# Another order of the units of a fused attention and gated-MLP kernel, with other PSUM tiles and copying engines

## The chip, the cores and the metric

One core of one Trainium2 chip runs the kernel. The metric is device time in microseconds (us); less is better. It has five instruction queues that matter here: TensorE (PE; PEld is its weight load), VectorE (DVE), ScalarE (ACT), GpSimd (POOL) and SyncE (SP, which only issues transfers). Each runs its own instructions in the order in which the program issues them.

## What is computed

An attention over blocks (batch 4, 8 heads, 768 rows in 8 blocks of 96, head size 64) is followed by a gated MLP with a spatial product. Cut to what matters:

```python
P = sort_net                                   # [4, 8, 8, 8]
for _ in range(5):                             # Sinkhorn rounds
    P = np.exp(P - np.max(P, axis=-1, keepdims=True))
    P = P / (np.sum(P, axis=-1, keepdims=True) + 1e-09)
    P = P / (np.sum(P, axis=-2, keepdims=True) + 1e-09)
k_sorted = np.einsum('bhij,bhjcd->bhicd', P, k_b)      # blocks mixed by P
v_sorted = np.einsum('bhij,bhjcd->bhicd', P, v_b)
attn = softmax(q_b @ k_sorted^T / 8)                   # each block with its own
x = (attn @ v_sorted), heads side by side              # [4, 768, 512]
h = np.maximum(x @ w_in, 0.0)                          # [.., 1024]
u, v = h[..., :512], h[..., 512:]
v_n = (v - mean(v)) / sqrt(var(v) + 1e-06)
v_s = np.einsum('ts,bsd->btd', w_spatial, v_n) + b_spatial[None, :, None]
out = (u * v_s) @ w_out                                # fp32
```

## The kernel before

The kernel is a list of small units. A table, ORDER (line 18 on), names them one after the other; `run` (line 806) takes each item, splits it at the colons and calls the function `u_<name>` with the rest as arguments. Nothing is scheduled afterwards: what a unit issues goes to its engines' queues in the order of the table. A unit on TensorE takes the number of a PSUM tile (`ps_tile`, line 110: 0 to 3 in use are pairs of banks, 10 to 17 are the single banks in these pairs) and a letter for the engine that copies its result away, D for VectorE and A for ScalarE. The next unit on the same tile waits for that copy.

The units, by what they do for one batch b (each batch goes through all of it; the table interleaves the MLP of one batch with the attention of the next):

- L loads q, k, v or a weight on GpSimd's queue (lines 177 to 194): `L:q:2:0:8` is q of batch 2, `L:wv` and `L:wu` are the two halves of w_in, `L:wsa` and `L:wsb` the row tiles 0 to 2 and 3 to 5 of w_spatial, `L:wo` is w_out; BI loads b_spatial spread over the partitions (line 206). Half of the first q comes in fp32 on SyncE's queue (LH, line 360) and is cast by QC (line 367).
- SK is a Sinkhorn round (lines 248 to 261): one exponential on ScalarE, six small steps on VectorE. PR, PC, P0 and PD spread its result into the mixing matrix pd.
- KT and VT mix k and v by it and turn them (L395); VM mixes v without a turn (L422), and VC copies vm to vb, one block a transfer, on SyncE's queue (L435); VB is the turn for batch 0.
- QT turns q on TensorE (L326). For batches 2 and 3, QP rearranges it (L377, a copy) and QX turns it with a transfer on SyncE's queue (L382).
- SC makes scores (L454) and their exponentials on ScalarE (L459); AT multiplies with v (L500) and divides on VectorE (L507, L508) into x. XT turns x on TensorE, XD with a transfer on SyncE's queue (L518).
- VP and VH make the v half of h for 128 rows (L567) with a relu (L128 or L130), ST its statistics (L587, L588), LN the root on ScalarE, LA the normalised v (L599). UP makes a piece of u (L613).
- WT and WW turn one and two row tiles of w_spatial (L536, L543). SP is the spatial product (L625, sum z with b_spatial on VectorE, L631), GT the product with u (L642, on VectorE or GpSimd), OP the output product (L651), OE its copy out of PSUM, OS the store (L666).
- SH, GH, OH, OI and OJ are the same steps in smaller pieces for the last batch (L681 to L719). CK and CF test whether the fast path's numbers were in range and write a flag; LF reads it into a register on every engine (L752). Behind the item IF stands a branch on it (line 815): the usual side runs the last output products, the other a safe path over everything.

`L:wsb` is thus needed first by the first WT or WW of a row tile from 3 to 5, `L:wu` by the first UP, and the whole of w_spatial and b_spatial by the first SP. What the reader has to know of the calls:

```python
for item in order.split():
    name, *args = item.split(":")
    units[name](*args)
```

Of the kernel before, what the change touches and what calls it, by code (L numbers as in the profile page):

```python
# [15 lines left out]


ORDER = """
S0 TB CO LH:S:0 L:q:0:4:8 SK:0 DM:10:3:384 DM:10:4:512 DM:10:13:512 BH ID IV:0 L:v:0:0:8 MC MA SK:1 DM:10:4:256 SK:2
QC:A:0 SK:3 SK:4 QC:A:1 QT:10:A:0:2 IV:2 QT:11:A:0:3 DM:12:4:512 QT:12:A:0:0 DM:13:10:192 PR:10 MB P0:0:2 P0:2:4  # L20
QT:11:D:0:1 VT:2:A:0:0 VT:3:D:0:1 PC:A P0:4:6 P0:6:8 VB:13:A:0:0 VB:12:D:0:1 L:k:0:0:8 VT:2:A:0:2 KT:3:D:0:1
KT:1:A:0:2 KT:0:A:0:3 VT:2:D:0:3 SC:3:0:1:1 KT:1:D:0:0 SC:0:0:2:0 VB:14:D:0:2 SC:3:0:3:0 L:k:1:0:8 AT:1:0:1:1
SC:0:0:0:0 L:v:1:0:8 PD:1:0:4 VB:15:D:0:3 SC:3:0:1:0 AT:1:0:2:0 SC:0:0:2:1 AT:2:0:3:0 SC:3:0:0:1 PD:1:4:8 AT:1:0:0:0
KT:0:A:1:0 XT:14:D:0:0:2 AT:3:0:0:1 SC:1:0:3:1 KT:0:A:1:3 AT:2:0:2:1 VM:1:A:1:0 AT:3:0:3:1 VM:0:A:1:1 VM:2:D:1:3
L:q:1:0:8 VM:1:A:1:2 XT:16:A:0:1:2 L:wv AT:0:0:1:0 XT:17:A:0:1:0 KT:2:D:1:1 KT:1:A:1:2 QT:16:D:1:1 QT:10:D:1:3
QT:11:A:1:2 QT:17:D:1:0 XT:14:D:0:0:0 SC:1:1:1:0 L:wsa SC:0:1:2:1 SC:3:1:2:0 VP:15:D:0:4 ST:0:4 VP:14:D:0:3 L:wu
SC:1:1:0:0 SC:0:1:1:1 VP:15:D:0:1 L:wsb ST:0:3 WT:16:A:1 WT:17:D:0 VP:14:A:0:0 ST:0:1 VH:15:A:0:2 ST:0:0 WT:16:A:2
VC:1:0:4 L:q:2:0:8 VH:17:A:0:5 VC:1:4:8 PD:2:0:4 ST:0:2 ST:0:5 AT:1:1:0:0 LN:0:0:6 AT:0:1:1:0 UP:2:A:0:0:0
UP:3:A:0:1:0 BI LA:0:3 LA:0:4 AT:1:1:2:0 SC:2:1:0:1 UP:0:A:0:1:1 LA:0:1 AT:3:1:2:1 L:v:2:0:8 WT:14:A:3 L:k:2:0:8
LA:0:5 LA:0:2 WW:1:D:4 LA:0:0 SC:0:1:3:1 SC:3:1:3:0 UP:2:A:0:0:1 PD:2:4:8 AT:0:1:3:1 QP:A:2:0 SP:1:0:3 QP:A:2:3  # L30
AT:3:1:3:0 QP:A:2:2 AT:2:1:0:1 QP:A:2:1 SP:0:0:0 AT:1:1:1:1 SP:3:0:2 VM:2:A:2:2 XD:1:0 VM:0:A:2:1 GT:D:0:0 SP:1:0:1
VM:3:D:2:0 GT:P:0:1 VM:2:A:2:3 VH:10:A:1:0 ST:1:0 KT:1:A:2:0 KT:2:D:2:1 KT:3:A:2:3 QX:2:0:4 KT:0:D:2:2 XD:1:1
UP:1:A:1:1:0 VH:16:D:1:1 SC:2:2:2:0 SC:0:2:0:0 VC:2:0:4:0:4 ST:1:1 GT:P:0:2 SC:1:2:3:0 VH:17:D:1:3 L:wo UP:2:A:1:1:1
AT:0:2:2:0 VH:16:A:1:4 AT:1:2:0:0 GT:P:0:3 VH:17:D:1:5 SC:2:2:1:0 L:q:3:0:8 SC:0:2:0:1 SC:1:2:1:1 VH:16:A:1:2 ST:1:3
UP:2:A:1:0:0 ST:1:5 AT:0:2:3:0 ST:1:4 ST:1:2 UP:1:A:1:0:1 LN:1:0:6 OP:3:0:2:2 LA:1:5 LA:1:1 SC:2:2:3:1 L:v:3:0:8
SC:0:2:2:1 PD:3:4:8 LA:1:0 OP:1:0:4:2 PD:3:0:4 LA:1:3 LA:1:2 OE:A:0:2 LA:1:4 L:k:3:0:8 QP:D:3:0 VC:2:4:8:0:4 OE:A:0:4
AT:2:2:3:1 SP:0:1:3 QP:A:3:3 AT:3:2:1:0 AT:1:2:2:1 QP:A:3:1 SP:2:1:1 AT:0:2:1:1 QP:A:3:2 VM:3:A:3:1 OP:1:0:0:2
OE:D:0:0 OS:0:0:0:1:A OS:0:0:1:2:A VM:2:A:3:3 AT:3:2:0:1 SP:0:1:2 VM:1:A:3:0 GT:P:1:1 XD:2:0 VM:3:D:3:2 SP:2:1:0
VH:16:D:2:2 QX:3:0:4 KT:0:A:3:0 KT:1:D:3:2 KT:2:D:3:3 KT:3:A:3:1 XD:2:1 VH:10:D:2:0 SC:1:3:0:1 ST:2:2 SC:3:3:0:0
SC:2:3:3:1 VC:3:4:8:0:4 OS:0:4:0:1 OS:0:4:1:2 VH:11:D:2:4 VH:10:A:2:5 AT:1:3:0:1 GT:P:1:3 VH:16:D:2:3 ST:2:3 ST:2:5  # L40
GT:P:1:2 SC:2:3:1:1 SC:0:3:2:1 SC:1:3:1:0 VH:17:A:2:1 GT:D:1:0 UP:2:A:2:1:0 AT:0:3:2:1 UP:1:A:2:1:1 ST:2:1 AT:3:3:1:1
ST:2:4 AT:2:3:3:1 UP:0:A:2:0:1 ST:2:0 UP:1:A:2:0:0 VC:3:0:4:0:4 AT:3:3:0:0 LN:2:0:6 LA:2:2 OP:0:1:0:2 OE:A:1:0 LA:2:4
AT:2:3:1:0 OP:1:1:4:2 LA:2:5 SC:3:3:2:0 LA:2:0 LA:2:3 LA:2:1 SC:0:3:3:0 OP:2:1:2:2 AT:3:3:3:0 SP:0:2:1 GT:D:2:1
OE:A:1:4 XD:3:1 AT:1:3:2:0 SP:3:2:0 SP:0:2:2 CK XD:3:0 GT:P:2:0 OE:A:1:2 SP:2:2:3 VH:1:D:3:5:3 GT:D:2:3 VH:10:D:3:4
UP:3:A:3:1:1 CF:11 VH:12:A:3:2 VH:13:A:3:1 OS:1:2:0:1 OS:1:2:1:2 LF VH:16:A:3:0 GT:D:2:2 OS:1:0:0:1:A OS:1:0:1:2:A
UP:2:A:3:1:0 ST:3:1 ST:3:3 UP:0:A:3:0:0 ST:3:4 ST:3:5 OP:1:2:0:2 ST:3:2 ST:3:0 OP:3:2:4:2 LN:3:0:6 LA:3:3 OE:D:2:0
LA:3:4 OP:2:2:2:2 LA:3:0 LA:3:1 OE:A:2:2 LA:3:5 UP:0:A:3:0:1 OE:A:2:4 LA:3:2 OS:0:2:0:1 OS:0:2:1:2 SH:12:3:2:0
SH:13:3:3:0 GH:P:3:3:0 SH:16:3:0:0 GH:D:3:2:0 SH:17:3:1:0 GH:P:3:0:0 SH:16:3:1:1 SH:12:3:2:1 OS:2:4 GH:P:3:1:0
SH:13:3:3:1 OS:2:0 GH:D:3:1:1 SH:17:3:0:1 OS:1:4 GH:D:3:3:1 OS:2:2 GH:P:3:0:1 GH:P:3:2:1 IF OH:16:3:2:0:512:0:4
OI:A:3:2:0:512 OH:12:3:3:0:512:0:4 OH:13:3:0:0:512:0:4 OI:D:3:0:0:512 OI:A:3:3:0:512 OH:17:3:1:0:512:0:4  # L50
OJ:3:2:0:512:S OJ:3:3:0:512:A OI:A:3:1:0:512 OJ:3:0:0:512:S OH:16:3:4:256:512:0:4 OI:D:3:4:256:512 OH:12:3:5:0:256:0:4
OI:D:3:5:0:256 OJ:3:1:0:512:S OJ:3:4:256:512:A OH:13:3:5:256:512:0:4 OJ:3:5:0:256:S OI:D:3:5:256:512
OH:17:3:4:0:128:0:4 OH:10:3:4:128:256:0:4 OI:B:3:4:0:256 OJ:3:5:256:512:A OJ:3:4:0:256:S
"""


# [792 lines left out]
```

## Time and profile before

| what | value |
|---|---|
| time, median of 3 runs | 150.17 us (149.5 to 150.21) |
| span of the profiled execution | 147.7 us, 4114 instructions |
| granted TensorE clock, mean | 1.000 |
| TensorE busy | 141.4 us, 96% of the span |
| VectorE / ScalarE / GpSimd busy | 115.1 / 85.2 / 39.1 us |
| chain that ended last, by engine | PE 82%, DMA 8%, DVE 5%, POOL 2% |
| read from HBM / written to it | 24.78 MB / 6.29 MB |

The page gives the profiled execution's span, from its first to its last instruction; the time of the runs has what lies around that too. The chain is followed back from the last instruction, at each step to what released it. Matmuls are pipelined, so a busy TensorE need not be at its peak. A load is told by its issue on the queue and by its time from there to landing.

### The profile page before, as it was taken

How to read it: one execution, taken by the hardware profiler on the slowest of the kernel's cores; microseconds unless marked ns; L12 is line 12 of the kernel's file. 1: busy time of each engine (PE TensorE's matmuls, PEld its weight loads, DVE VectorE, ACT ScalarE, POOL GpSimd, SP SyncE). 2: the span in 40 equal slices, each digit the busy share in tenths (PEclk: the TensorE clock that was granted, in tenths of full speed). 3: DMA queues.
4: the chain of work that ended last, by engine and by line, in shares of the span. 5: the costliest groups of instructions: out<-in, count | busy, mean ns of one | idle time of the engine just before them, and what ended most of it. 6: DMA issues, size and time to landing. Idle time of an engine off the chain costs nothing.

```text
span 147.7 us, 4114 instructions
## 1 busy us (share of the span) xinstructions
PE 141.4 (96%) x1691; PEld 101.0 (68%) x1691; DVE 115.1 (78%) x263; ACT 85.2 (58%) x125; POOL 39.1 (26%) x44
## 2 busy tenths in 40 slices
...
GB/s 60 278 204 205 204 207 201 208 225 243 227 233 231 204 200 269 131 177 211 206 202 175 213 239 278 132 0 83 28 0 60 190 2 284 0 2 266 307 210 228
DMA packets 37013, 25.93 MB, mean 176 GB/s; under 512 B 16704, under 2 KB 34112, under 8 KB 36992
## 3 DMA queue, kind: packets, MB, share of 16 engines
...
HBM read 24.78 MB, written 6.29 MB: 210 GB/s over the span
## 4 chain that ended last, share of the span: by engine, by line
PE 82%; DMA 8%; DVE 5%; POOL 2%; issue 1%; ACT 1%; POOLq 0%; DVEq 0%
PE ps L625 16%; PE ps L567 15%; PE ps L613 14%; PE ps L651 11%; DMA k_in<-in_k_dram 8%; PE ps L681 5%; PE ps L500 4%; PE ps L395 4%; PE ps L701 4%; PE ps L454 4%; PE ps L422 3%; DVE x_sb L508 2%; PE ps L326 1%; PE ps L536 1%; PE ps L530 1%; DVE vb L124 1%
## 5 line engine op out<-in xcount | busy, mean ns | idle before, releaser
L642 POOL TENSOR_TENSOR gt<-z,u_sb 128x768 bf16<-128x768 f32 x7 | 11.4, 1642 | 68.0 <-DVE z L631 54.7
L459 ACT ACTIVATE ex_all<-ps 96x768 bf16<-96x768 f32 x32 | 23.7, 805 | 5.0 <-PE ps L454 4.1
L625 PE MATMUL ps<-wspT,v_sb 128*128 128x384 bf16 x144 | 25.0, 326 | 0.0
L567 PE MATMUL ps<-w_in_sb,xT 128*128 128x256 bf16 (+1 forms) x176 | 23.8, 283 | 0.0
L613 PE MATMUL ps<-xT,w_in_sb 128*128 128x384 bf16 x128 | 23.0, 326 | 0.0
L128 ACT ACTIVATE u_sb<-ps 128x768 bf16<-128x768 f32 x16 | 13.0, 811 | 17.3 <-PE ps L613 17.2
L508 DVE TENSOR_TENSOR x_sb<-ps,rec_all 96x512 bf16<-96x512 f32 x32 | 22.0, 687 | 1.1
L625 PEld LDWEIGHTS <-v_sb 128*128 128x128 bf16 x144 | 13.5, 98 | 8.4
L567 PEld LDWEIGHTS <-xT 128*128 128x128 bf16 x176 | 16.2, 98 | 4.0
L651 PE MATMUL ps<-w_out_sb,gt 128*128 128x256 bf16 x144 | 16.9, 273 | 0.0
L613 PEld LDWEIGHTS <-w_in_sb 128*128 128x128 bf16 x128 | 12.0, 98 | 7.0
L587 DVE BATCH_NORM_STATS2 stats<-v_sb 128x6 f32<-128x512 bf16 x24 | 16.2, 675 | 0.6 <-ACT v_sb L128 0.5
L122 ACT COPY o_sb<-ps 128x1024 f32<-128x1024 f32 (+2 forms) x11 | 8.9, 830 | 12.6 <-PE ps L701 9.3
L631 DVE TENSOR_TENSOR z<-ps,b_bc 128x768 f32<-128x768 f32 x12 | 11.5, 954 | 5.9 <-PE ps L625 5.1
L651 PEld LDWEIGHTS <-gt 128*128 128x128 bf16 x144 | 13.8, 98 | 2.0
L500 PEld LDWEIGHTS <-ex_all 96*128 96x128 bf16 x256 | 11.1, 97 | 2.6
L500 PE MATMUL ps<-vb,ex_all 96*128 96x65 bf16 x256 | 12.4, 193 | 0.1
L122 ACT CAST vm<-ps 128x768 bf16<-128x768 f32 x9 | 6.8, 807 | 9.7 <-PE ps L422 6.6
L694 POOL TENSOR_TENSOR gt<-z,u_sb 128x512 bf16<-128x512 f32 (+1 forms) x5 | 5.2, 1046 | 21.5 <-DVE z L687 21.5
L507 DVE RECIPROCAL rec_all<-ps 96x8 f32<-96x8 f32 x32 | 6.3, 196 | 5.5 <-PE ps L500 5.3
L130 DVE TENSOR_SCALAR v_sb<-ps 128x512 bf16<-128x512 f32 (+1 forms) x12 | 8.7, 727 | 1.7 <-PE ps L567 1.5
L236 PE MATMUL ps<-warm 128*128 128x512 bf16 (+3 forms) x38 | 8.5, 386 | 1.3 <-DVE warm L210 1.3
...
## 6 DMA issues: line engine op xcount, KB each, us to landing
v_in<-in_v_dram POOLq DMA_DIRECT2D x4, 768.0 KB, 16.0
k_in<-in_k_dram POOLq DMA_DIRECT2D x4, 768.0 KB, 14.9
vb<-vm SPq DMA_DIRECT2D x24, 99.0 KB, 4.8
q_in<-in_q_dram POOLq DMA_DIRECT2D x3, 768.0 KB, 11.6
...
out_dram<-o_sb SPq DMA_DIRECT2D x4, 512.0 KB, 5.9
...
ws_in<-in_moe_w_spatial_dram POOLq DMA_DIRECT2D x2, 576.0 KB, 18.9
```

The lines of the kernel that those rows point to most:

```text
L122: nc.scalar.copy(out=out, in_=in_)
L128: nc.scalar.activation(out=out, in_=in_, func=AF.Relu)
L459: nc.scalar.activation(out=e_tile(b, hp, ih).rearrange("p h (x g) -> p h x g", g=G), in_=t[0:BLK, :, 0:HW].rearrange("p h (g x) -> p h x g ...
L500: nc.tensor.matmul(t[:, hh, ii * VW:ii * VW + D + 1], lhsT=e[:, c:c + 128], rhs=vb[b % 2][:, ih * NI + ii, 2 * hp + hh, 0:D + 1], start=Tr ...
L508: nc.vector.tensor_mul(out=x_sb[:, hp].rearrange("p i (h d) -> p h i d", h=2), in0=tv[:, :, :, 0:D], in1=_raw_ap(rec, 0, [rec.ap[0], [NI, ...
L567: nc.tensor.matmul(t[:, x, c:c + DH // parts], lhsT=st["xT", b][:, n // 3, kc, (n % 3) * 128:(n % 3 + 1) * 128], rhs=w_in_sb[:, kc, DH + c ...
L587: nc.vector.bn_stats(out=stats, in_=st["v_sb", b, n])
L613: nc.tensor.matmul(t[:, x, 0:HW], lhsT=w_in_sb[:, kc, mc * 128:(mc + 1) * 128], rhs=st["xT", b][:, ih, kc, :], start=(kc == 0), stop=(kc = ...
L625: nc.tensor.matmul(t[:, x, 0:HW], lhsT=st["v_sb", b, n][:, mc * 128:(mc + 1) * 128], rhs=wspT[:, 3 * x:3 * x + 3, n, :], start=(n == 0), s ...
L631: nc.vector.tensor_add(out=z.rearrange("p (x c) -> p x c", x=2), in0=t[:, :, 0:HW], in1=b_bc.rearrange("p (x c) -> p x c", x=2),)
L642: eng.tensor_mul(out=gt, in0=st["z", b, mc], in1=u)
L651: nc.tensor.matmul(t[:, x, c:c + w], lhsT=st["gt", b, mc][:, (n0 + x) * 128:(n0 + x + 1) * 128], rhs=w_out_sb[:, mc, c:c + w], start=(mc = ...
```

## The change

The change rewrites the table ORDER and nothing else: the same 385 items, with the same work in each, in another turn, with other tile numbers and other letters for the copying engine. Counted over the table, the two casts QC go from ScalarE to VectorE; VectorE copies four of the eight QP (one before), three of the sixteen UP (none), seven VH (nine), four VM (three), and six KT (seven); GpSimd multiplies ten of the twelve GT (seven) and three of the eight GH (five). The table fills most of the diff; this is its core, with the QC casts, the first u unit (UP) and the first use of `L:wsb` (WW in the new table, WT:14:A:3 in the old one, a little ahead of WW there):

```diff
@@ -16,41 +16,41 @@
...
-QC:A:0 SK:3 SK:4 QC:A:1 QT:10:A:0:2 IV:2 QT:11:A:0:3 DM:12:4:512 QT:12:A:0:0 DM:13:10:192 PR:10 MB P0:0:2 P0:2:4
...
-SC:1:1:0:0 SC:0:1:1:1 VP:15:D:0:1 L:wsb ST:0:3 WT:16:A:1 WT:17:D:0 VP:14:A:0:0 ST:0:1 VH:15:A:0:2 ST:0:0 WT:16:A:2
-VC:1:0:4 L:q:2:0:8 VH:17:A:0:5 VC:1:4:8 PD:2:0:4 ST:0:2 ST:0:5 AT:1:1:0:0 LN:0:0:6 AT:0:1:1:0 UP:2:A:0:0:0
...
+QC:D:0 SK:3 QT:12:A:0:3 QC:D:1 SK:4 IV:2 DM:12:4:512 QT:16:A:0:2 DM:13:10:192 QT:14:A:0:1 PR:10 MB P0:2:4 P0:0:2
...
+VP:15:A:0:3 SC:1:1:2:0 SC:0:1:0:0 ST:0:3 SC:3:1:1:1 WT:14:D:2 VP:15:D:0:0 PD:2:0:4 WT:13:A:1 ST:0:0 VH:11:A:0:2
+AT:2:1:3:0 AT:3:1:2:0 UP:0:A:0:0:1 AT:1:1:1:0 PD:3:4:8 VH:15:A:0:5 ST:0:2 QP:D:2:2 L:wsb VP:17:A:0:1 ST:0:5 SC:2:1:2:1
...
+WW:2:A:4 LA:0:4 AT:3:1:0:1 WT:11:D:3 LA:0:0 WT:10:A:0 UP:1:A:0:1:0 BI LA:0:2 QP:A:2:1 AT:3:1:2:1 L:k:2:0:8 AT:2:1:0:0
...
```

The first place is GpSimd's queue, from the two loads of w_spatial to the k of batch 2 (ws_in is half of w_spatial, L185 the u half of w_in, q_in, v_in and k_in are those of batch 2, pd is the mixing matrix):

```order
 L191 DMA ws_in<-in_moe_w_spatial_dram 128x3x768
 L185 DMA w_in_sb<-in_moe_w_in_dram 128x4x512
+L177 DMA q_in<-in_q_dram 128x8x384
+L293 TENSOR_TENSOR pd<-mask_89,prep_sb 128x512 x2
 L191 DMA ws_in<-in_moe_w_spatial_dram 128x3x768
-L177 DMA q_in<-in_q_dram 128x8x384
 L293 TENSOR_TENSOR pd<-mask_89,prep_sb 128x512
+L177 DMA v_in<-in_v_dram 128x8x384
 L206 DMA b_bc<-in_moe_b_spatial_dram 128x768
-L177 DMA v_in<-in_v_dram 128x8x384
 L177 DMA k_in<-in_k_dram 128x8x384
```

The load of q of batch 2 moved from behind the second half of w_spatial to ahead of it, and v of batch 2 from behind b_spatial to ahead of it.

The second place is SyncE's queue around the transfers of batch 2 (xT is the turned x of batch 1, qT the turned q of batch 2, the copies to vb above it are those of batch 1, those below of batch 2):

```order
 L435 DMA vb_98<-vm 96x1x528 x8
-L518 DMA_TRANSPOSE xT<-x_sb 128x16x96
+L518 DMA_TRANSPOSE xT<-x_sb 128x16x96 x2
 L382 DMA_TRANSPOSE qT<-qp 128x24x128
-L518 DMA_TRANSPOSE xT<-x_sb 128x16x96
 L435 DMA vb_97<-vm 96x1x528 x8
```

The second half of xT moved from behind qT to ahead of it. Within the eight copies to vb, which read alike here, the blocks 4 to 7 now stand ahead of 0 to 3 (`VC:2:4:8` ahead of `VC:2:0:4` in the table).

The third place is TensorE's queue where it reads the flag. Before, that stood among the v projections of batch 3:

```order
L567 MATMUL ps<-w_in_sb,xT 128x256
L567 LDWEIGHTS xT
L752 TENSOR_LOAD flag
L567 MATMUL ps<-w_in_sb,xT 128x256
L567 LDWEIGHTS xT
```

and now it stands behind the last spatial product (L681); the branch follows, and behind the branch the listing goes on with the safe path:

```order
L681 LDWEIGHTS v_sb
L681 MATMUL ps<-wspT,v_sb 128x256
L752 TENSOR_LOAD flag
L815 COMPARE_AND_BRANCH
L267 LDWEIGHTS spread
```

The read of the flag moved from between matmuls to the place directly ahead of the branch.

More of the change, by code (lines that the diff above doesn't have):

```diff
@@ L29 @@
[L29 to L53, printed above, removed]
+S0 TB L:q:0:4:8 CO LH:S:0 SK:0 DM:10:3:384 DM:10:4:512 DM:10:13:512 BH ID IV:0 MC MA SK:1 L:v:0:0:8 DM:10:4:256 SK:2
@@ new lines @@
+QC:D:0 SK:3 QT:12:A:0:3 QC:D:1 SK:4 IV:2 DM:12:4:512 QT:16:A:0:2 DM:13:10:192 QT:14:A:0:1 PR:10 MB P0:2:4 P0:0:2
+VT:3:A:0:1 VT:1:D:0:0 QT:14:A:0:0 PC:A L:k:0:0:8 VB:16:A:0:1 P0:6:8 P0:4:6 VB:17:D:0:0 KT:1:A:0:2 VT:0:D:0:2
+KT:3:A:0:1 L:k:1:0:8 KT:2:D:0:0 KT:1:D:0:3 SC:0:0:1:1 L:v:1:0:8 VT:3:A:0:3 VB:15:D:0:2 SC:0:0:2:0 AT:1:0:1:1
+SC:3:0:3:0 PD:1:0:4 VB:14:D:0:3 PD:1:4:8 SC:0:0:0:0 AT:1:0:2:0 SC:3:0:3:1 AT:2:0:3:0 KT:0:A:1:1 AT:1:0:0:0 SC:3:0:0:1
+SC:2:0:2:1 VM:0:D:1:1 VM:3:A:1:0 XT:12:D:0:0:2 VM:2:A:1:3 AT:0:0:0:1 VM:1:A:1:2 VC:1:0:4 AT:3:0:2:1 L:q:1:0:8
@@ new lines @@
+AT:2:0:3:1 KT:0:A:1:3 L:wv XT:12:D:0:1:0 SC:3:0:1:0 QT:13:D:1:0 QT:11:D:1:2 VC:1:4:8 KT:2:A:1:0 QT:10:D:1:3 KT:3:A:1:2
+QT:13:D:1:1 L:wsa L:wu XT:12:A:0:1:2 AT:0:0:1:0 SC:2:1:3:0 SC:3:1:1:0 L:q:2:0:8 VP:13:D:0:4 XT:11:D:0:0:0 ST:0:4
+VP:15:A:0:3 SC:1:1:2:0 SC:0:1:0:0 ST:0:3 SC:3:1:1:1 WT:14:D:2 VP:15:D:0:0 PD:2:0:4 WT:13:A:1 ST:0:0 VH:11:A:0:2
+AT:2:1:3:0 AT:3:1:2:0 UP:0:A:0:0:1 AT:1:1:1:0 PD:3:4:8 VH:15:A:0:5 ST:0:2 QP:D:2:2 L:wsb VP:17:A:0:1 ST:0:5 SC:2:1:2:1
+SC:1:1:3:1 SC:0:1:0:1 PD:2:4:8 L:v:2:0:8 ST:0:1 LN:0:0:6 UP:3:A:0:0:0 AT:2:1:1:1 UP:1:A:0:1:1 LA:0:5 LA:0:3 LA:0:1
@@ new lines @@
+WW:2:A:4 LA:0:4 AT:3:1:0:1 WT:11:D:3 LA:0:0 WT:10:A:0 UP:1:A:0:1:0 BI LA:0:2 QP:A:2:1 AT:3:1:2:1 L:k:2:0:8 AT:2:1:0:0
+SP:0:0:2 QP:A:2:0 VM:1:A:2:1 XD:1:0 AT:3:1:3:1 XD:1:1 SP:2:0:0 GT:P:0:0 VM:3:A:2:2 QP:D:2:3 VM:1:D:2:3 SP:0:0:1
+VM:2:D:2:0 SP:1:0:3 KT:2:A:2:0 QX:2:0:4 KT:0:D:2:3 KT:3:D:2:1 KT:1:D:2:2 VC:2:4:8:0:4 VH:15:D:1:0 VH:14:A:1:3
+VH:10:D:1:5 VC:2:0:4:0:4 VH:17:D:1:1 SC:2:2:3:0 ST:1:5 ST:1:3 SC:0:2:3:1 SC:1:2:1:1 ST:1:1 UP:3:D:1:0:1 VH:15:A:1:4
+VH:13:A:1:2 SC:2:2:0:0 ST:1:4 ST:1:0 GT:P:0:1 PD:3:0:4 SC:0:2:1:0 AT:3:2:1:1 UP:1:A:1:1:1 ST:1:2 L:wo LN:1:0:6
@@ new lines @@
+UP:2:A:1:1:0 GT:P:0:3 GT:P:0:2 AT:3:2:3:1 AT:0:2:3:0 UP:1:D:1:0:0 LA:1:2 LA:1:4 L:k:3:0:8 SC:3:2:2:0 SC:2:2:0:1 LA:1:1
+LA:1:5 OP:0:0:2:2 OE:A:0:2 L:q:3:0:8 SC:1:2:2:1 QP:A:3:3 AT:3:2:0:0 LA:1:0 L:v:3:0:8 LA:1:3 OP:2:0:4:2 AT:0:2:1:0
+AT:3:2:0:1 SP:1:1:2 OE:A:0:4 QP:D:3:2 AT:2:2:2:0 AT:3:2:2:1 SP:0:1:1 XD:2:0 QP:D:3:0 QP:A:3:1 VM:1:D:3:2 XD:2:1
+SP:2:1:0 VM:3:A:3:0 VM:0:A:3:1 OP:1:0:0:2 KT:0:A:3:2 OE:D:0:0 GT:P:1:1 QX:3:0:4 VM:2:A:3:3 SP:3:1:3 VH:10:A:2:2
+VC:3:0:4:0:4 KT:2:D:3:1 KT:1:A:3:0 KT:3:A:3:3 VH:10:D:2:4 SC:1:3:1:0 ST:2:2 SC:2:3:0:0 SC:3:3:3:0 VH:11:D:2:3 ST:2:3
```

21 lines of the change are left out of this document (14 added, 7 removed).

## The prediction

> **What bounds the kernel now.** I read the page first, then the sums by stage, then the chain of waits, and last the loads and their times to landing. Every number is a time in us from the span's start unless it is said to be a length.
>
> The page's first part gives TensorE's share of the span:
>
> ```profile
> PE 141.4 (96%) x1691; PEld 101.0 (68%) x1691; DVE 115.1 (78%) x263; ACT 85.2 (58%) x125; POOL 39.1 (26%) x44
> ```
>
> The view of sums by stage splits this into a start and a body (columns: length, busy time of each engine, clock, DMA share, GB/s):
>
> ```profile
> 12.00:24.80 12.80, 11.74 (x284) 9.60 (x282) 11.93 (x24) 11.43 (x17) 9.24 (x11) 1.00 1.32 204
> 24.80:50.00 25.20, 25.15 (x361) 18.01 (x361) 21.96 (x50) 21.85 (x33) 2.27 (x3) 1.00 1.23 225
> ```
>
> Up to 24.8 three engines are nearly full, VectorE and ScalarE among them. From there TensorE is busy for 25.15 of 25.20, at the full granted clock, while the DMA engines stay just as full (share over 1). So two resources run side by side: TensorE, and the stream of loads that GpSimd issues. The chain of waits, in order of time (start, length, what), shows which of them decides:
>
> ```profile
> 3.90 11.51 DMA k_in<-in_k_dram
> ...
> 24.85 0.48 PE ps L422 x2
> ...
> 37.04 0.87 PE ps L567 x8
> ...
> 38.40 2.60 PE ps L613 x16
> ...
> 43.17 0.34 PE ps L536 x6
> ...
> 46.27 1.95 PE ps L625 x12
> ...
> 68.99 1.30 PE ps L613 x8
> 70.29 1.75 PE ps L651 x16
> 72.03 0.45 PE ps L454 x16
> 72.48 1.85 PE ps L651 x16
> 74.34 0.24 PE ps L500 x8
> ...
> 144.43 0.02 issue
> ```
>
> The wait for the first k ends at 3.90 + 11.51 = 15.4. From 24.85 to 144.43 each piece is a matmul piece of TensorE that begins where the last ended. Both orders issue the same matmuls, so after 24.85 the old order has nothing to give back: a new order can win only in the first 24.85 us or in the 3.3 us behind 144.43 (147.7 less 144.43), and it loses wherever TensorE comes to a unit whose data are not there. That is the whole calculation: for each load, the time when it lands, and the time at which the new order comes to its first user.
>
> **Loads of the weights and of batch 2.** These are GpSimd's issues of the u half of w_in (L185), the second half of w_spatial (L191) and q of batch 2 (L177):
>
> ```profile
> 18.59 0.81 POOL L185 DMA_DIRECT2D w_in_sb<-in_moe_w_in_dram  x1
> 19.38 0.76 POOL L191 DMA_DIRECT2D ws_in<-in_moe_w_spatial_dram  x1
> 20.12 0.94 POOL L177 DMA_DIRECT2D q_in<-in_q_dram  x1
> ```
>
> and this is how long each took from issue to landing, in the same order:
>
> ```profile
> w_in_sb<-in_moe_w_in_dram POOLq DMA_DIRECT2D x1, 512.0 KB, 19.3
> ws_in<-in_moe_w_spatial_dram POOLq DMA_DIRECT2D x1, 576.0 KB, 21.9
> q_in<-in_q_dram POOLq DMA_DIRECT2D x1, 768.0 KB, 25.0
> ```
>
> So they landed at 18.59 + 19.3 = 37.9, 19.38 + 21.9 = 41.3 and 20.12 + 25.0 = 45.1: one behind the other in the order of issue, 3.4 us for the second and 3.8 for the third, although they were issued within 2 us. A load's landing is set by what stands ahead of it in the stream. The change leaves the u half in its place and puts q of batch 2 ahead of the second half of w_spatial. I estimate from these rows that the u half still lands at 37.9, q at 41.7 (37.9 + 3.8), and the second half of w_spatial at 45.1, since the three are the same bytes.
>
> First users. The old order begins its first u unit (L613) at 38.40, half a microsecond behind the landing. The new one has two v projections (L567, 0.87 each) and one turn of w_spatial (L536, 0.34) less ahead of its first u unit; at the old pace it is there at 38.40 - 2.08 = 36.3, and stands still until 37.9: 1.6 late. The old order uses the second half of w_spatial first at 43.17 (L536), 1.9 behind the landing. The new one has two score units more ahead of that (0.45 for two, L454) and one turn less: 43.17 + 0.45 - 0.34 = 43.3, against a landing at 45.1: 1.8 late. The second wait holds the first (TensorE that is already 1.6 late waits only 0.2 more there), so they are one term: **1.8**. Its bounds: 1.6 if the first use of w_spatial is not late at all, and 2.3 if VectorE also stands in the way. For the change puts a cast of q of batch 2 on VectorE (unit QP, L377) as soon as that load is due. VectorE then waits for 41.7, and queued behind it are the cast, two statistics and one attention result, which frees the PSUM tile that the turn of w_spatial needs:
>
> ```profile
> L587 DVE BATCH_NORM_STATS2 stats<-v_sb 128x6 f32<-128x512 bf16 x24 | 16.2, 675 | 0.6 <-ACT v_sb L128 0.5
> L508 DVE TENSOR_TENSOR x_sb<-ps,rec_all 96x512 bf16<-96x512 f32 x32 | 22.0, 687 | 1.1
> L124 DVE COPY qp<-q_in 128x768 bf16<-128x768 bf16 x1 | 0.4, 358 | 0.0
> ```
>
> 41.7 + 0.36 + 2 x 0.68 + 0.69 = 44.1, and with the small instructions between them close to 45.1: the late load covers this wait, and 0.5 is my allowance where the cover is thin. The vector b and v of batch 2 change places as well; the first user of either comes behind 45.1 by at least one spatial unit (1.95), and I cost that swap at nothing, hidden behind the same wait.
>
> **The transfers of batch 2 on SyncE.** The change puts both transposes of x (L518) ahead of the transpose of q (L382), and the copies vm to vb (L435) of blocks 4 to 7 ahead of 0 to 3. Old times on SyncE's queue (the x8 row is all eight copies, the last row the eighth), and the eighth's time to landing:
>
> ```profile
> 51.80 4.27 SPq L382 DMA_TRANSPOSE qT<-qp  x1
> 57.59 5.70 SPq L435 DMA_DIRECT2D vb<-vm  x8
> 62.30 0.99 SPq L435 DMA_DIRECT2D vb<-vm  x1
> vb<-vm SPq DMA_DIRECT2D x1, 99.0 KB, 7.7
> ```
>
> So the last copy landed at 62.30 + 7.7 = 70.0, and its group was first used at 74.34 (L500). The new order comes to the same blocks' place in the queue, now 0 to 3, with less done: one attention unit (0.24), one u unit (1.30), three scores (0.67) and two output units (1.75 + 1.85), together 5.8. At the old pace that is 68.5. If the copies landed as before, this is 1.5 late, less than the 1.8 already lost, and costs nothing. But they start later. The new q transpose waits for its last cast on VectorE, and that stands behind the sum z of the second spatial unit:
>
> ```profile
> L631 DVE TENSOR_TENSOR z<-ps,b_bc 128x768 f32<-128x768 f32 x12 | 11.5, 954 | 5.9 <-PE ps L625 5.1
> ```
>
> The first spatial unit was at 46.27; the new one has two attention units more ahead of it (0.5) and is 1.8 late: 48.6. Two spatial units and some 0.6 of small units later it is 53.1; z 0.95 and the cast 0.36 give 54.4, the q transpose 4.27 more: the copies start at 58.7, not 57.59, 1.1 later. Landing 1.1 later, at 71.1, is 2.6 late at 68.5: **0.8** more than the 1.8. Bounds: 0, and as the other end the copies of batch 1, which ran wholly beside loads:
>
> ```profile
> 27.67 5.21 SPq L435 DMA_DIRECT2D vb<-vm  x8
> vb<-vm SPq DMA_DIRECT2D x1, 99.0 KB, 8.8
> ```
>
> There the eighth, issued at the end of that row less about 0.6, or 32.3, landed at 41.1, 13.4 after the first issue; 58.7 + 13.4 = 72.1 would be 3.6 late, 1.8 more than the first term. I take 0.8 because the same transfer of the same batch is the nearest row.
>
> **The start and the flag.** The casts of the first q go from ScalarE to VectorE, between the rounds of the Sinkhorn chain:
>
> ```profile
> 8.00 0.21 DVE L249 TENSOR_REDUCE rowsum<-p_all 32x8 f32<-32x64 f32 x1 [0.32 <-ACT p_all L248]
> ...
> 11.51 0.28 PE L267 MATMUL ps<-p_t,spread 32*128 32x64 bf16 x4 [0.52 <-DVE mask L224]
> ...
> L124 DVE CAST kt_all<-ps 128x768 bf16<-128x768 f32 x7 | 6.5, 947 | 0.5 <-PE ps L395 0.4
> ```
>
> VectorE idles 0.32 per round there. A cast of this shape on it lies between the 0.36 of the bf16 copy above and this 0.95 from PSUM, so two of them push the chain back by 0.1 to 1.3 in all. I take nothing for it: k lands at 15.4, and the chain ends ahead of 11.51, where L267 reads it, 3.9 earlier; if k were there at once, the cost would be these 0.1 to 1.3.
>
> The read of the flag (L752) moves from between matmuls to the last place before the branch, on TensorE too, where the output matmuls (L701) follow. What it costs between matmuls is the difference of these two runs of the same 24, without and with it:
>
> ```profile
> 115.53 2.62 PE ps L567 x24
> ...
> 119.54 2.73 PE ps L567 x24
> ```
>
> That is 0.11. VectorE, which had nothing queued ahead, lost 0.67 between writing the flag and its next instruction:
>
> ```profile
> 120.90 0.96 DVE L642 TENSOR_TENSOR gt<-z,u_sb 128x768 bf16<-128x768 f32 x1 [0.67 <-DVE flag L749]
> ```
>
> With the branch right behind it TensorE can run ahead less, so I take 0.2, near the TensorE row, with 0.1 and 0.67 as ends. The Trainium skill (DMA: Bandwidth & Descriptors, Latency and other measured facts) puts the floor of a tensor_load at about 600 ns. By that figure the flag term would be 0.6 and the sum 0.4 more; VectorE's 0.67 agrees with it and TensorE's 0.11 does not.
>
> **All other moves.** The remaining units keep their work and change their turn, their PSUM tile and some of them the copying engine: three relus of u go to VectorE, and GpSimd multiplies ten of the twelve z in place of seven. By the page VectorE is busy for 78% of the span, ScalarE for 58% and GpSimd for 26%, and TensorE's work hides theirs, so I cost these at nothing. Where that cover is gone, a PSUM tile comes free later by one copy, about 0.95.
>
> **The sum.** 1.8 + 0.8 + 0.2 = 2.8 on the profiled span of 147.7, or 150.5. The median of the runs, 150.17, lies 2.5 above that span; I add the 2.8 to it: **153.0**.
>
> **Rivals.** A measurement of this kernel can tell about 0.5% from no change, or 0.75 us.
> *Only the loads count.* If the copies vm to vb land as early as before, the second term is nothing: 1.8 + 0.2, or 152.2. For it: the 4.3 us between the last landing at 70.0 and its old use at 74.34. Chance 0.20.
> *The copies crowd.* All eight now run beside the load of w_out, as those of batch 1 ran beside loads: 1.8 + 1.8 + 0.67 = 4.3, or 154.4. Chance 0.15.
> *No change.* The profiled execution may have had slower loads than the timed ones. If the stream is 1.8 ahead of this trace at 45.1 (4%), no unit waits for it, and what is left is the flag: 0.2, or 150.4. Against it: the DMA share is full in the profile, and a full stream has no reserve to run on. This is also the case in which the change does not do what it says, since an order for late loads should put a load's user later, and the first u unit comes earlier. Chance 0.15.
> *Faster.* With loads that early the start decides: from 15.4 to 24.85 VectorE is the fullest engine, and the new order does all of q's turns of batch 0 on ScalarE:
>
> ```profile
> L124 DVE COPY qT<-ps 128x768 bf16<-128x768 bf16 x4 | 2.0, 546 | 0.0
> ```
>
> One such copy and one later turn of x of like size off that stretch would end it 1.1 earlier: 150.17 - 1.1 + 0.2 = 149.3. It decides only once the u half lands by 36.3 and the second half of w_spatial by 43.3. Chance 0.05.
>
> **How the numbers follow.** The forecast has 0.45, with its own range from 152.7 to 153.9 (2.5 and 3.8, by the ends of its first and last term); together with the two slower rivals slower has 0.80, no change 0.15, faster 0.05. The range runs from 150.4, the flag alone, to 154.9, the sum of all upper ends (2.3 + 1.8 + 0.67 = 4.8, over the median); outside it lie the faster case and a part of no change.
>
> **What would show it.** Right: a wait of TensorE for the u half of w_in or for ws_in between 36 and 46, landings of these at about 37.9 and 45.1 with q between, and the first spatial unit at about 48.6; then L500 held back near 70 by a copy to vb. Wrong: ws_in landing before 43.5, TensorE without a wait in that stretch, or the first spatial unit before 47; a flag term over 0.3 would show as a gap between L681 and L701.

## The result, and the profile after

| | time, median (all runs) | ratio to the kernel before, 95% interval |
|---|---|---|
| kernel before, beside it | 150.15 us (149.5 to 150.21, 4 runs) | |
| kernel after | 153.34 us (153.24 to 154.01, 4 runs) | 1.0242 [1.0205, 1.0279] |
| kernel after, in a later set of runs | 153.36 us (153.16 to 154.39, 6 runs) | 1.0234 [1.0177, 1.0291] |

The change makes the kernel 3.2 us slower by the medians and 3.6 (3.1 to 4.2) by the ratio; 153.0 (150.4 to 154.9) was forecast. The ratios and their intervals leave out executions that ran longer at a lower granted clock, the medians do not, so the cost of an edit is given below by its ratio. The profiled execution of before was its fastest (149.5), that of after its slowest (154.01), so the two pages differ by 4.5 and 1.3 of that is the spread of executions. The second profile of the same kernel, of a run of 153.16 with a span of 151.4, is called "after again" below.

The first rows of the page of after:

```profile
span 152.2 us, 4122 instructions
PE 142.9 (94%) x1689; PEld 100.8 (66%) x1691; DVE 117.3 (77%) x269; ACT 80.3 (53%) x118; POOL 42.4 (28%) x45
```

**The loads.** GpSimd's issues of the u half of w_in, of q of batch 2 and of the second half of w_spatial, from the timeline, then the time of each from issue to landing:

```profile
20.62 0.82 POOL L185 DMA_DIRECT2D w_in_sb<-in_moe_w_in_dram  x1
21.41 0.92 POOL L177 DMA_DIRECT2D q_in<-in_q_dram  x1
...
31.92 0.81 POOL L191 DMA_DIRECT2D ws_in<-in_moe_w_spatial_dram  x1
```

```profile
w_in_sb<-in_moe_w_in_dram POOLq DMA_DIRECT2D x1, 512.0 KB, 16.9
q_in<-in_q_dram POOLq DMA_DIRECT2D x1, 768.0 KB, 20.9
ws_in<-in_moe_w_spatial_dram POOLq DMA_DIRECT2D x1, 576.0 KB, 13.3
```

They land at 37.5, 42.3 and 45.2, where 37.9, 41.7 and 45.1 had been forecast. But TensorE does not stand still for them here. It is late before it comes there, from the start on. The start on TensorE's timeline (idle time ahead of a group, and what ended it, in brackets):

```profile
10.01 1.02 PE L236 MATMUL ps<-warm 128*128 128x512 bf16 x4 [0.89 <-ACT qT L122]
...
12.81 0.28 PE L267 MATMUL ps<-p_t,spread 32*128 32x64 bf16 x4
...
16.88 0.53 PE L395 MATMUL ps<-pd,k_in 128*64 128x128 bf16 x12 [0.64 <-DVE pd L281]
```

Warming matmuls (L236) share a PSUM bank with a turn of q whose copy on ScalarE they wait for; two of the three turns of q that stand ahead of L267 now come behind that wait, and L267 comes at 12.81 in place of 11.51 (11.90 in after again); and the first k unit waits for pd until 16.88, not for k, which had landed at 15.3. Further on, TensorE stops once with no releaser, in the midst of a score unit:

```profile
31.69 0.26 PE L454 MATMUL ps<-qT,kt_all 64*128 64x96 bf16 x4
32.60 0.43 PE L454 MATMUL ps<-qT,kt_all 64*128 64x96 bf16 x12 [0.65 <-issue]
```

So it reaches the first turn of the second half of w_spatial (L543) at 45.50. VectorE's timeline shows how near the second suspect of the prediction is, the cast that waits for q:

```profile
42.41 0.36 DVE L124 COPY qp<-q_in 128x768 bf16<-128x768 bf16 x1 [0.20 <-DMA q_in<-in_q_dram]
...
44.71 0.69 DVE L508 TENSOR_TENSOR x_sb<-ps,rec_all 96x512 bf16<-96x512 f32 x1
```

VectorE frees the PSUM tile of that turn at 44.71 + 0.69 = 45.4. Three things end within 0.3 of each other: TensorE's own lateness (45.5), the landing (45.2), and VectorE (45.4).

**The copies to vb.** SyncE's eight issues, and the eighth (issued at 63.5) to its landing; then the first L500 behind that time on TensorE:

```profile
58.57 5.54 SPq L435 DMA_DIRECT2D vb<-vm  x8
```

```profile
vb<-vm SPq DMA_DIRECT2D x1, 99.0 KB, 6.1
```

```profile
70.63 0.65 PE L500 MATMUL ps<-vb,ex_all 96*128 96x65 bf16 x16
```

They start at 58.57 (58.7 forecast) and the last lands at 69.7 (71.1 forecast): nobody waits. Its first user is the second of the two attention units in the L500 row.

**The tail.** This was priced at 0.2 for the flag. GpSimd, VectorE and TensorE at the last products:

```profile
140.87 2.16 POOL L694 TENSOR_TENSOR gt<-z,u_sb 128x512 bf16<-128x512 f32 x2 [1.12 <-DVE z L687]
142.43 0.69 DVE L687 TENSOR_TENSOR z<-ps,b_bc 128x512 f32<-128x512 f32 x1 [1.04 <-POOL gt L694]
142.49 0.33 PEld L701 LDWEIGHTS <-gt 128*128 128x128 bf16 x3 [0.20 <-issue]
142.50 0.82 PE L701 MATMUL ps<-w_out_sb,gt 128*128 128x512 bf16 x3
...
143.91 1.25 PE L701 MATMUL ps<-w_out_sb,gt 128*128 128x512 bf16 x5 [0.59 <-DVE gt L694]
```

At the flag it is TensorE's weight loads that stand still for 0.20; its matmuls show no idle time there (the L701 row of PE has no bracket), and the first L701 starts 0.20 behind the last L681, where the matmuls ahead of it start 0.11 apart. So the flag costs TensorE at most 0.1 here, not the 0.2 of the forecast, and in after again the distance is 0.11, which is nothing. But VectorE idles 1.04 until GpSimd is done with a product, and the fourth output matmul (L701) waits 0.59 for what VectorE makes after that. In the kernel before, TensorE had no wait in this stretch. The chain of waits also has GpSimd's own read of the flag ahead of that product:

```profile
141.40 0.42 POOLq L752
141.83 0.58 POOL gt L694
```

So a part of this wait may be the flag's; the runs do not separate them.

### The profile page after: what moved, and what is told of

It reads as the page before. It is cut to its first block, busy times and chain, and to the rows that moved or that the text cites. A ratio compares the mean times of both kernels' runs of the same rounds, so it can differ in the third digit from the quotient of the medians.

```text
span 152.2 us, 4122 instructions
## 1 busy us (share of the span) xinstructions
PE 142.9 (94%) x1689; PEld 100.8 (66%) x1691; DVE 117.3 (77%) x269; ACT 80.3 (53%) x118; POOL 42.4 (28%) x45
## 5 line engine op out<-in xcount | busy, mean ns | idle before, releaser
L642 POOL TENSOR_TENSOR gt<-z,u_sb 128x768 bf16<-128x768 f32 x10 | 17.1, 1718 | 68.0 <-DVE z L631 65.1
L625 PE MATMUL ps<-wspT,v_sb 128*128 128x384 bf16 x144 | 24.9, 326 | 0.0
L613 PE MATMUL ps<-xT,w_in_sb 128*128 128x384 bf16 x128 | 23.1, 326 | 0.0
L567 PE MATMUL ps<-w_in_sb,xT 128*128 128x256 bf16 (+1 forms) x174 | 23.0, 281 | 0.1
L625 PEld LDWEIGHTS <-v_sb 128*128 128x128 bf16 x144 | 13.7, 98 | 8.7
L122 ACT COPY o_sb<-ps 128x1024 f32<-128x1024 f32 (+2 forms) x10 | 8.1, 808 | 19.0 <-PE ps L701 14.6
L128 ACT ACTIVATE v_sb<-ps 128x512 bf16<-128x512 f32 (+1 forms) x14 | 8.8, 630 | 16.8 <-PE ps L567 16.8
L587 DVE BATCH_NORM_STATS2 stats<-v_sb 128x6 f32<-128x512 bf16 x24 | 16.2, 676 | 0.9 <-ACT v_sb L128 0.8
L631 DVE TENSOR_TENSOR z<-ps,b_bc 128x768 f32<-128x768 f32 x12 | 11.5, 958 | 6.8 <-PE ps L625 6.7
L613 PEld LDWEIGHTS <-w_in_sb 128*128 128x128 bf16 x128 | 11.7, 98 | 6.9
L128 ACT ACTIVATE u_sb<-ps 128x768 bf16<-128x768 f32 x13 | 10.4, 806 | 3.2 <-PE ps L613 3.1
L500 PE MATMUL ps<-vb,ex_all 96*128 96x65 bf16 x256 | 11.8, 193 | 0.3 <-ACT o_sb L122 0.3
L500 PEld LDWEIGHTS <-ex_all 96*128 96x128 bf16 x256 | 10.4, 97 | 2.4 <-issue 0.5
L236 PE MATMUL ps<-warm 128*128 128x512 bf16 (+3 forms) x38 | 9.4, 413 | 2.2 <-DVE warm L210 1.3
L293 POOL TENSOR_TENSOR pd<-mask,prep_sb 128x512 bf16<-128x512 bf16 x6 | 6.6, 1103 | 17.1 <-ACT prep_sb L122 9.6
L122 ACT CAST kt_all<-ps 128x768 bf16<-128x768 f32 x10 | 7.7, 800 | 6.4 <-PE ps L395 6.4
```

The costliest lines, as they stand in the source:

```text
L122: nc.scalar.copy(out=out, in_=in_)
L128: nc.scalar.activation(out=out, in_=in_, func=AF.Relu)
L500: nc.tensor.matmul(t[:, hh, ii * VW:ii * VW + D + 1], lhsT=e[:, c:c + 128], rhs=vb[b % 2][:, ih * NI + ii, 2 * hp + hh, 0:D + 1], start=Tr ...
L567: nc.tensor.matmul(t[:, x, c:c + DH // parts], lhsT=st["xT", b][:, n // 3, kc, (n % 3) * 128:(n % 3 + 1) * 128], rhs=w_in_sb[:, kc, DH + c ...
L587: nc.vector.bn_stats(out=stats, in_=st["v_sb", b, n])
L613: nc.tensor.matmul(t[:, x, 0:HW], lhsT=w_in_sb[:, kc, mc * 128:(mc + 1) * 128], rhs=st["xT", b][:, ih, kc, :], start=(kc == 0), stop=(kc = ...
```

## The experiments

The theory of the prediction is the **loads theory**: the order of the loads holds TensorE at 37.9 and 45.1, and the start costs nothing. Its rival out of the profile after is the **start theory**: the start (and the stop at 31.7) cost the time, and the landings are beside the point.

### Either part alone, and both, on the kernel before

One line moved, the load of q of batch 2:

```diff
-VP:15:D:0:1 L:wsb ST:0:3
+VP:15:D:0:1 L:q:2:0:8 L:wsb ST:0:3
...
-VC:1:0:4 L:q:2:0:8 VH:17:A:0:5
+VC:1:0:4 VH:17:A:0:5
```

> The kernel before with only the load of q of batch 2 put ahead of the second half of w_spatial on GpSimd's queue. That half should land at 45.1 in place of 41.3, and its first user, the turn of its first row tile (L536), was at 43.17. Loads theory and start theory alike: TensorE waits 1.8 there, and 152.0. If the profile's loads were slow ones and the stream has a reserve (the rival of no change): 150.2 to 150.7 and a landing before 43.5.

Measured: 151.71 beside 149.8 of the kernel before, ratio 1.0148 [1.0109, 1.0187]. TensorE's timeline at that turn:

```profile
45.16 0.51 PE L536 MATMUL ps<-ident,ws_in 128*128 128x128 bf16 x6 [1.39 <-DMA ws_in<-in_moe_w_spatial_dram]
```

The mechanism of the first term is real, and this one swap costs 2.2 (1.6 to 2.8 by the interval; the forecast was 1.8). A landing is set by what stands ahead in GpSimd's queue, and TensorE has no reserve behind it.

The new start alone (items up to the second VB of batch 0):

```diff
-QC:A:0 SK:3 SK:4 QC:A:1 QT:10:A:0:2 IV:2 QT:11:A:0:3 DM:12:4:512 QT:12:A:0:0 DM:13:10:192 PR:10
+QC:D:0 SK:3 QT:12:A:0:3 QC:D:1 SK:4 IV:2 DM:12:4:512 QT:16:A:0:2 DM:13:10:192 QT:14:A:0:1 PR:10
...
```

> The kernel before with only the new order's start, that is its items up to the second VB of batch 0 (the q casts on VectorE, the turns of q on ScalarE, the dummies on the bank of a turn); everything behind as before. The loads theory (the prediction: start and q casts cost nothing, the order of the loads costs 1.8): no change, 150.2, and the first KT (L395 from k) at 15.5 as before. The start theory (the start costs TensorE 1.4 to 2.3 and the loads' landings are only a floor that this hides): first KT at 16.5 to 17 and 151.6 to 152.5.

Measured: 150.45, ratio 1.0054 [1.0034, 1.0074]. The start is not free, but alone it costs 0.8 (0.5 to 1.1) and not 1.4 to 2.3. Both theories had it wrong.

Both together:

> The kernel before with both edits that were run alone: the new order's start (alone 150.45) and q of batch 2 loaded ahead of the second half of w_spatial (alone 151.71, beside 149.8 for the kernel before). If the landings hide what the start loses, as the prediction has it: 151.7 to 151.9, and the wait of L536 for ws_in is shorter by what the start lost. If both are paid in full: 152.4.

Measured: 151.85, ratio 1.0126 [1.0092, 1.0159]. The two do not add up: 2.2 and 0.8 alone, 1.9 (1.4 to 2.4) together, which is the cost of the swap. TensorE's wait for the landing, 1.4 with the swap alone, is shorter by 0.5:

```profile
PE ps L536 <- DMA ws_in<-in_moe_w_spatial_dram: 0.9, 1, 0.9
```

So behind the swap nothing is to be paid for the start, and not because k lands late, as the prediction had it, but because the landing at 45.1 holds TensorE up in any case.

### Undoing parts of the kernel after

The old start in the kernel after (the diff above, the other way round):

> The kernel after with the old order's start up to the second VB of batch 0, everything behind as after. Loads theory: no change from after, 153.3, with TensorE waiting at the first u unit for a landing at 37.6 and at the first turn of the second half of w_spatial for 45.2. Start theory: the start gains 1.4 to 2.3, but the same landings hold TensorE at a lag of 1.8, so only about 0.5 of it is left: 152.8. If the landings are no floor at all: 151.0 to 151.9.

Measured: 153.5, ratio 1.0267 [1.0226, 1.0309]: no gain. The loads theory said so. Of the two waits that it expected the trace shows one: the weight load of L543 waits 0.50 for the landing at 45.2. At the first u unit TensorE came too late to wait, for two other waits had held it up before, the stop and one for v of batch 1 (L422), which the new order uses earlier and which the prediction did not look at:

```profile
PE ps L422 <- DMA v_in<-in_v_dram: 0.9, 1, 0.9
PE ps L454 <- issue: 0.8, 1, 0.8
```

The loads undone, the start kept:

```diff
-SC:3:1:1:0 L:q:2:0:8 VP:13:D:0:4
+SC:3:1:1:0 L:wsb L:q:2:0:8 VP:13:D:0:4
...
-AT:3:1:2:0 UP:0:A:0:0:1 AT:1:1:1:0 PD:3:4:8 VH:15:A:0:5 ST:0:2 QP:D:2:2 L:wsb VP:17:A:0:1
+AT:3:1:2:0 AT:1:1:1:0 PD:3:4:8 VH:15:A:0:5 ST:0:2 VP:17:A:0:1
...
-LN:0:0:6 UP:3:A:0:0:0
+LN:0:0:6 UP:0:A:0:0:1 UP:3:A:0:0:0
...
-VM:3:A:2:2 QP:D:2:3
+VM:3:A:2:2 QP:D:2:2 QP:D:2:3
```

> The kernel after with the loads taken out as a cause: the second half of w_spatial is loaded ahead of q of batch 2 again, the first u unit comes one u unit's place later, behind the landing of the u half, and the first q cast of batch 2 (which would stand on VectorE waiting for q) goes beside the last. Loads theory: 1.8 of the loss is gone, 151.5. Start theory: TensorE is already 2.3 late there and waited for neither, so no change, 153.3.

Measured: 157.23, ratio 1.0498 [1.0466, 1.053]; the waits show new obstacles:

```profile
PE ps L613 <- ACT ex_all L459: 2.2, 1, 2.2
...
PE ps L625 <- DVE vm L124: 1.0, 1, 1.0
```

The first u unit, put behind a score unit on its own PSUM tile, waits 2.2 for that unit's exponential on ScalarE, and the fourth spatial product 1.0 for VectorE, where the late q cast now crowds. The profiled execution took 159.92, and behind the wait of 2.2 its granted clock fell as well (last section), so its lengths do not add up to the median. The edit made new waits and tells nothing about the loads.

The stop at 31.7: more and smaller warming matmuls, so that everything behind stands later in TensorE's instruction stream.

```diff
-DM:10:4:256
+DM:10:16:64
...
-DM:12:4:512
+DM:12:16:128
...
-DM:13:10:192
+DM:13:30:64
```

> The kernel after with three groups of warming matmuls at the start cut into smaller ones of the same columns (4 of 256 into 16 of 64, 4 of 512 into 16 of 128, 10 of 192 into 30 of 64): 44 instruction pairs more on TensorE ahead of the rest, so that everything behind stands 44 pairs later in its instruction stream. In the kernel after TensorE stands still for 0.8 from 31.74 on in the midst of a score unit, with no releaser. If that is the instruction stream being loaded too late at a fixed count: the gap moves to another unit, ahead of 31, or goes; the second half of w_spatial still holds TensorE at 45.2, so the time falls by no more than 0.4, to 152.9 to 153.3. If the gap belongs to the data of that unit: it stays where it is.

Measured: 154.64, ratio 1.0302 [1.0264, 1.034]. The stop is gone from that score unit, and no new one of its kind stands ahead of 45, so it hangs on the place in the instruction stream and not on the unit's data. It gained nothing. TensorE now comes early enough to be caught by the other half of the prediction's first term, VectorE behind q (which landed at 42.8 in this run):

```profile
42.89 0.36 DVE L124 COPY qp<-q_in 128x768 bf16<-128x768 bf16 x1 [1.10 <-DMA q_in<-in_q_dram]
```

```profile
45.73 0.83 PE L543 MATMUL ps<-ident,ws_in 128*128 128x128 bf16 x12 [0.49 <-DVE x_sb L508]
```

That it is 1.3 slower than the kernel after is explained by this row only for 0.5. In the profiled execution another part lies at the very end: its last output matmul starts at 148.33 (148.43 in after), but its last store lands at 151.98 (151.24 in after). Why is open.

q of batch 3 ahead of k of batch 3, for in the kernel after its cast waited until 78.2 and held ScalarE's copies:

```diff
-LA:1:4 L:k:3:0:8 SC:3:2:2:0
+LA:1:4 L:q:3:0:8 L:k:3:0:8 SC:3:2:2:0
...
-OE:A:0:2 L:q:3:0:8 SC:1:2:2:1
+OE:A:0:2 SC:1:2:2:1
```

> The kernel after with q of batch 3 loaded ahead of k of batch 3 again, as the order before has it. If the late q of batch 3 (landed 78.2, and the cast of it held ScalarE and behind it a copy out of PSUM) is what took 0.3 to 0.6 between 73 and 87: 152.8 to 153.0. If it is hidden: 153.3.

Measured: 153.38, ratio 1.0234 [1.0196, 1.0272]: it is hidden, and this guess fell.

The rotating z buffers of the tail:

```diff
-st["z", b, mc, c] = z = moe.tile([128, S], FP32, name="z", tag="z", bufs=NZ)[:, 0:w]
+st["z", b, mc, c] = z = vt_all.rearrange("p a c -> p (a c)")[:, 0:1024].bitcast(FP32) if (mc, c) == (3, 0) else moe.tile([128, S], FP32, name="z", tag="z", bufs=NZ)[:, 0:w]
```

> The kernel after with one z of the tail (output tile 3, first 512 tokens) in a place of its own, the idle vt buffer, in place of the third of the rotating z buffers. The fourth output matmul (L701) waited there for z, and z for GpSimd's product that still read the same buffer. The buffer theory: the wait of L701 of 0.6 goes, and the time falls by 0.6 to 0.7 to 152.6. If the engine behind is as late anyway (VectorE must make two products and two sums in that stretch): a change of 0.2 or less.

Measured: 153.12, ratio 1.0223 [1.0185, 1.0262]. In the trace the wait is gone:

```profile
140.68 0.69 DVE L687 TENSOR_TENSOR vt_all<-ps,b_bc 128x512 f32<-128x512 f32 x1
...
141.79 2.55 PE L701 MATMUL ps<-w_out_sb,gt 128*128 128x512 bf16 x11
```

VectorE makes that sum without idling, and TensorE runs through its output matmuls, although the flag is read as late as in after. The profiled span is 150.9 against 151.4 of after again. In the medians only 0.2 of it is to be seen, less than they tell apart: the wait is shown, its worth in time is not.

### Repairing all at once, and the flag

Three kernels beside each other: after again; "no loads repaired", that is after with the old start, the shifted stream, the z of its own and the flag read early again; and "all repaired", the same with the loads in the old order, `QP:D:2:2` beside `QP:A:2:1` and the first u unit behind `VH:15:A:0:5`.

> The kernel after once more, beside the three others on the same chip: 153.2 to 153.6, with the first turn of the second half of w_spatial (WW, L543) at 45.2 to 45.6 and 0.6 of waiting at the fourth output matmul (L701).

> The kernel after with everything repaired that was found besides the loads: the old start, the shifted instruction stream, the z of its own in the tail, and the flag read early again (behind an output product of batch 2, some 10 ahead of the branch). The order of the loads stays as in after. Loads theory: TensorE is held at 45.2 by the second half of w_spatial and by VectorE's wait for q of batch 2, 2.1 behind the old pace, and later pieces of some 0.4 stay: 152.2 to 152.6. If the start and the gap were the cause and the loads only stood beside them: 151 or less.

> The same, and the loads repaired as well: the second half of w_spatial ahead of q of batch 2, the first q cast of batch 2 on VectorE ten units later, behind the landing of q, and the first u unit one v projection later. Loads theory: the first turn of the second half of w_spatial (L543) starts ahead of 44.7, and what is left is the wait of the new order's early VM for v of batch 1 (landing 23.9 to 24.5, 1.3 behind the old pace): 0.8 less than without the loads' repair, 151.4 to 151.8. If the loads are no cause: as without it, 152.2 to 152.6.

Measured, in this order: 153.36, as expected; 154.39, ratio 1.0284 [1.0217, 1.0352]; 154.79, ratio 1.0279 [1.0184, 1.0374]. None of the forecast gains came, and the fastest executions of the two repaired kernels are alike (153.11 and 153.09). The traces say more. "No loads repaired" is the kernel after without the late start and without the stop, and there the two waits of the prediction stand in the open:

```profile
37.82 0.99 PE L613 MATMUL ps<-xT,w_in_sb 128*128 128x384 bf16 x5 [0.44 <-DMA w_in_sb<-in_moe_w_in_dram]
```

```profile
45.23 0.12 PEld L543 LDWEIGHTS <-ws_in 128*128 128x128 bf16 x2 [0.78 <-DMA ws_in<-in_moe_w_spatial_dram]
45.26 0.22 PE L543 MATMUL ps<-ident,ws_in 128*128 128x128 bf16 x1 [0.41 <-DVE x_sb L508]
```

The first u unit waits for the u half, and L543 for the landing and for VectorE. How far each kernel lies behind the old pace at a place (its start there, less the time at which before's profiled execution had the same TensorE work left; good to some 0.1). Old start and no loads repaired were profiled in executions of 152.98 and 153.44, 0.5 and 0.9 below their medians; the table holds for the executions in it:

| place on TensorE | after | after again | old start | z of its own | no loads repaired |
|---|---|---|---|---|---|
| L267 starts at | 12.81 | 11.9 | 11.5 | 12.2 | 11.5 |
| score unit at 31, behind by | 1.9 | 1.6 | 1.2 | 1.5 | 1.3 |
| the next score unit | 2.5 | 2.2 | 1.9 | 2.2 | 1.0 |
| first L625 starts at | 48.87 | 48.62 | 48.62 | 48.62 | 48.62 |
| there behind by | 2.3 | 2.1 | 2.1 | 2.1 | 2.1 |
| last k unit (L395) of batch 3 | 3.3 | 2.6 | 2.6 | 2.7 | 3.0 |
| first L681 | 3.4 | 2.7 | 2.7 | 2.8 | 3.1 |
| last L701 | 4.2 | 3.5 | 3.5 | 2.8 | 3.6 |

The first spatial product starts at 48.62 in four of five, to the hundredth, with starts that differ by 0.7, and never earlier; the prediction's time for it was 48.6. Two more kernels with this order of the loads stand at 49.10 (shifted stream, held by VectorE) and 49.14 (q of batch 3 moved). So the landing at 45.2 is a floor: with the old start and in no loads repaired the weight load of L543 waits for it (0.50 and 0.78), with the z of its own for 0.17. In after again TensorE comes just as the half has landed (45.12), and in after 0.3 later, held up as much by what lies ahead: the start, the wait for v of batch 1 (0.6 in after again) and the stop. In after the time has two sufficient causes, and neither can be read off as the one.

"All repaired" does not answer its question. Its second half of w_spatial landed at 41.3 and nothing waited for it, but TensorE was 2.6 behind by the score unit at 31. k of batch 0 landed at 16.3, and behind that wait the clock fell. Columns: stretch, length, then busy time (and count) of PE, PEld, DVE, ACT and POOL, granted clock, DMA share, GB/s:

```profile
12.00:14.00 2.00, 1.24 (x36) 1.03 (x33) 1.84 (x4) 1.54 (x3) 0.00 (x0) 1.00 1.32 209
14.00:16.00 2.00, 1.05 (x16) 0.88 (x15) 1.51 (x4) 1.04 (x2) 1.89 (x2) 1.00 1.31 200
16.00:18.00 2.00, 1.66 (x32) 1.66 (x34) 0.20 (x2) 0.76 (x1) 2.00 (x4) 0.55 1.31 204
18.00:20.00 2.00, 2.00 (x44) 1.75 (x42) 1.68 (x2) 0.83 (x2) 2.00 (x3) 0.59 1.31 203
```

So what the kernel after would take with its loads repaired and a good start stays open; the fastest execution at 153.09, for which there is no trace, speaks against a large gain. And the early flag was no repair: TensorE waits for it between an output product and L681 in both,

```profile
PE ps L681 <- issue: 0.4, 1, 0.4
```

The flag alone, on the kernel before:

```diff
-OS:1:2:1:2 LF VH:16:A:3:0
+OS:1:2:1:2 VH:16:A:3:0
...
-SH:17:3:0:1 OS:1:4 GH:D:3:3:1
+SH:17:3:0:1 OS:1:4 LF GH:D:3:3:1
```

> The kernel before with the read of the flag moved, on every engine, from among the v projections of batch 3 to behind the last spatial product, right ahead of the branch. The prediction's term: 0.2 (0.1 to 0.7), a gap of TensorE of 0.2 between L681 and L701, 150.1 to 150.3 beside 149.9 to 150.1. The figure of the Trainium skill's page DMA: Bandwidth & Descriptors (about 600 ns for a tensor_load): 0.6.

Measured: 150.73 beside 149.97, ratio 1.0047 [1.0013, 1.0081], with both kernels' lowest runs at 149.41. Its profiled execution, of 149.44 one of its fastest, has a span of 147.6 (147.7 before) and no gap between the two lines:

```profile
137.33 1.80 PE L681 MATMUL ps<-wspT,v_sb 128*128 128x256 bf16 x15
138.97 1.89 PE L701 MATMUL ps<-w_out_sb,gt 128*128 128x512 bf16 x8
```

This trace says that nothing was lost, the runs together say 0.7 (0.2 to 1.2), which would fit the 0.6 better than the 0.2. Which of them is right was not settled.

## Why the prediction was right

**The bound.** It was read rightly: from 24.85 on the old order had nothing to give back, so the new one could only lose where it came to data too early. It lost.

**The first term, 1.8 (1.6 to 2.3).** Right in place and mechanism: the landings came at the forecast times, the swap alone costs 2.2 (1.6 to 2.8) on the kernel before, and the new order is 2.1 behind at the first spatial product. The 0.3 more is not VectorE's: in the four kernels with 48.62, L543 begins within 0.14 of the landing, and in no loads repaired, where it waits for VectorE as well, that wait ends with the landing. The allowance of 0.5 for VectorE showed in one kernel, the shifted stream, where L543 waited for x_sb until 45.73 and the first spatial product came at 49.10. But the sign given for the term failed in after itself, which the prediction would have had to call wrong: TensorE has no wait there, since a start, a wait for v of batch 1 and a stop that were priced at nothing or not seen had made it late by the same amount. The experiments show that the landing alone suffices, not that it alone held after.

**The second term, 0.8.** Wrong. The issues began as worked out (58.57 for 58.7), but the step "landing 1.1 later, at 71.1" failed: the eighth copy took 6.1 to land where the row of before had 7.7, and TensorE came to the L500 row of its first user at 70.6, 0.9 behind the landing. The time to landing beside other loads did not carry over from one order to the next.

**The start.** The amount, 0, was right for the kernel as a whole, the reason wrong. The step that failed is "k lands at 15.4, and the chain ends ahead of 11.51, 3.9 earlier": between 11.51 and the first k unit lie P0, the copy to prep_sb and the v units, which read pd as well and do not wait for k. So the cover was not 3.9, and the first k unit waited for pd. Alone the start costs 0.8, inside the bounds of 0.1 to 1.3 that were written down for the case without cover.

**The flag, 0.2.** Not confirmed. In the traces the move costs TensorE's matmuls 0.1 (after) or nothing (after again, and alone on the kernel before), in the runs alone 0.7 (0.2 to 1.2). The Trainium skill's 600 ns (DMA: Bandwidth & Descriptors, Latency and other measured facts) would be too much for the traces and would fit the runs. TensorE's load itself took 0.49 in before, 0.79 in the kernel with the flag alone moved, 0.99 in after and 1.08 where I put it between other matmuls; what of it is seen depends on what is queued.

**All other moves, nothing.** Wrong by about 1.3, beside the wait for v of batch 1, which the first term covers. The tail lost 0.8 in the trace to one z that got a buffer from which GpSimd was still reading: VectorE's and GpSimd's averages said that there was cover, but a buffer of three knows no average. A further 0.5 in after again (1.0 in after) came between the first spatial product and the last k unit of batch 3. In after 0.3 of it is a wait of L500 for ScalarE's copy of an output product out of PSUM; that wait is gone with q of batch 3 moved, but so it is in after again, and the time did not change. The cause of the rest stays open.

So the sum, 2.8, came near the measured 3.2 to 3.6 with one term right (1.8, measured 2.1), one at nothing instead of 0.8, one unconfirmed (0.2), and 1.3 in the trace where nothing had been forecast. That the misses nearly cancel is luck. The nearest rival by mechanism was "only the loads count".
